# A scan and two MLPs in one kernel: the first units in another form, scores in quarters, a new opening order

## The chip, the cores and the metric

The kernel runs on one core of a Trainium2 chip. The metric is the device time of one execution in microseconds (us). The engines are named as in the profile: PE is TensorE, DVE is VectorE, ACT is ScalarE, POOL is GpSimd, SP is SyncE; SP issues the DMAs of this kernel.

## The reference

Four batches, eight heads, 768 time steps, 48 features a head. A gated linear scan is followed by two MLPs, each over 3072 tokens of 384 features with 2048 hidden features; everything is fp32.

```python
f = 1.0 / (1.0 + np.exp(-f_logit))
for t in range(S):
    state = f[:, :, t, :, None] * state + np.einsum('bhd,bhe->bhde', k[:, :, t], v[:, :, t])
    y[:, :, t] = np.einsum('bhd,bhde->bhe', q[:, :, t], state)
x = y.transpose(0, 2, 1, 3).reshape(B * S, H * D)
x = np.square(np.maximum(x @ w_in, 0)) @ w_out
h = x @ w_in2
out = (h * np.tanh(softplus(h))) @ w_out2
```

## The kernel before

**The scan** is cut into 12 chunks of 64 steps. A *unit* is one chunk of two of the four batches, so there are 24 units, two to a chunk; four units make a block of 512 tokens. Unit i and unit i + 2 follow each other in time, and the state goes from one to the next. The two batches of a unit are its two halves y; queries, keys and gates lie with features on the partitions, rows 64 to 111 for the one half and 0 to 47 for the other, and heads by time in the columns (8 x 64 = 512).

The steps of a unit, each a small function: load_j, load_f and load_v bring the gate logits, keys and queries, and values. v_min (L443), a_exp and a_ln (L446, L450), v_scan (L454) and a_dq, a_dk (L459, L464) make the decay factors. v_q (L469) scales the queries, one half at a time, into the tile mv; v_k (L473) scales the keys in place; v_end (L477) keeps the decay over the chunk. m_a (L488, L489) computes the scores, keys against queries, for 8 heads and 2 halves: 32 matmuls with 48 rows into a PSUM tile at. v_mask (L542) multiplies one half of them by the causal mask, into mv. m_t (L530) transposes the keys and a_kn (L552) copies them into kns, behind rows that hold a unit matrix (eye_kn, L651); thus one matmul takes the state and the new keys together. m_y (L567) makes the output y of the unit, features by tokens, in 64 matmuls; a_x (L603) rounds it to fp32r as the high part of x, v_x (L607) subtracts and keeps the rest as the low part. m_u (L577, L578) makes the new state, v_s (L593) scales it by the decay and puts it into the rows of the values tile vs of unit i + 2. From unit 9 on (QUAD) scores and states are made in another arrangement, quarters_a (L500, tile aq) and quarters_u (L511): two heads lie one above the other, so that four matmuls of 64 columns stand side by side, and the scores take two PSUM buffers; v_mask (L539) then takes four instructions of 64x4x64.

**The MLPs** work in fp32r with every operand split in a high and a low part, and three products (high by high, high by low, low by high). One step fc of 16 takes 128 hidden features of a block: l1 (L351) is 9 matmuls of 128x512 into an h buffer, act_a (L747, L748, L370) makes relu squared and its high part gh, act_b (L375) the low part gl, l2 (L362) is 9 matmuls into three accumulators. l2 of a step comes two steps of l1 later. There are 96 steps for each MLP; h_p has 5 PSUM buffers with the tag h, which l1, scores, y, states and transposed keys share. The weights of the first MLP come as 64-bit floats (load_w) and are turned by w_top or a_top, w_f (L271), w_hi (L292) and w_lo (L297). m_warm (L615) issues matmuls on constants into an accumulator.

**The order of the work.** Each engine works through its own list in the order in which the program issues instructions, and a semaphore holds it where it needs another engine. From the start to step 18 of l1 the order is the string START, a list of the functions above written by hand; hold makes the next load wait for the DVE instruction issued last. After that run(i) issues, for step i, what put(step, priority, function) has filed for it, sorted by priority, lower first. do_l1 has priority 100 and do_l2 120, v_x 13 and act_b 32 in the first 80 steps.

**The end.** Two sums tell whether the fast path is valid: set_flag_sum (L797 to L801, two small matmuls, a reduction and a comparison) writes flag. At the end every engine loads it (L90) and branches (L91) over a slow path that is not executed here. The results of the last block are stored by L880, L882 and L884.

Of the kernel before, what the change touches and what calls it, by code (L numbers as in the profile page):

```python
# [50 lines left out]
w_lo 1; do_l1 1; v_s 2 0; w_hi 2; act_a 0; w_f 3; w_lo 2; w_hi 3; act_b 0; hold; load_w 7; a_exp 4; w_lo 3; w_top 4;
w_top 5; hold; load_f 6; act_a 1; do_l1 2; w_f 4; a_ln 4; do_l2 0; v_s 2 1; act_a 2; w_f 5; hold; load_v 4; act_b 1;
v_s 3 0; hold; load_v 5; v_min 5; w_hi 4; v_s 3 1; do_l1 3; a_exp 5; w_lo 4; v_scan 4; a_top 6; act_b 2; w_f 6;
do_l2 1; w_hi 5; v_min 6; do_l1 4; w_lo 5; hold; load_f 7; do_l2 2; act_a 3; act_b 3; a_ln 5; act_a 4; w_top 8;
a_dq 4; do_l1 5; v_scan 5; do_l2 3; w_hi 6; a_top 7; v_q 4 0; a_dq 5; w_lo 6; act_b 4; hold; load_w 10; a_dk 4;
load_w 9; do_l1 6; w_f 7; a_dk 5; v_q 4 1; a_exp 6; w_hi 7; act_a 5; v_q 5 0; hold; load_v 6; do_l2 4; w_lo 7; v_k 4;
w_f 8; v_k 5; m_t 4; act_a 6; a_ln 6; w_hi 8; w_top 10; act_b 5; v_q 5 1; m_a 4; w_top 9; v_mask 4 1; w_lo 8; m_t 5;
do_l1 7; a_kn 4; m_a 5; act_a 7; v_min 7; v_end 5; v_end 4; v_scan 6; do_l1 8; a_dq 6; a_dk 6; v_mask 4 0; hold;
load_v 7; do_l2 5; m_u 4; a_exp 7; w_f 9; v_mask 5 1; a_kn 5; m_y 4; act_b 6; do_l2 6; w_f 10; act_a 8; v_mask 5 0;
a_ln 7; w_hi 10; v_s 4 0; w_hi 9; load_w 12; act_b 7; v_q 6 1; a_top 11; v_q 6 0; m_y 5; a_x 5; v_k 6; v_s 4 1; a_x 4;  # L60
# [917 lines left out]
```

## Time and profile before

| | |
|---|---|
| median of 3 runs | 885.54 us (885.53 to 886.3) |
| profiled execution, its own time | 883.13 us |
| its span | 881.3 us |
| PE busy | 867.0 us, 98% |
| DVE busy | 665.7 us, 76% |
| ACT busy | 634.0 us, 72% |
| POOL busy | 7.9 us, 1% |
| granted clock, mean | 0.997 |
| DMA | 90.79 MB, mean 103 GB/s |
| first group of L351 | starts at 34.18 us |
| last group, L872 | starts at 871.20 us |

Times in the views are us from the start of the span, of one profiled execution. Its own time is 1.8 us above its span, and 2.4 us below the median of the runs. Matmuls overlap: one of 512 columns is listed with 0.39 us, while nine that follow each other take 2.04.

### The profile page before, as it was taken

What the parts mean: (1) busy time and instruction counts of PE and PEld (TensorE: products, weight loads), DVE (VectorE), ACT (ScalarE), POOL (GpSimd) and SP (SyncE); (2) the same over time, 40 slices, a digit from 0 to 9 for tenths busy, and PEclk for the clock granted to TensorE, in tenths of its full rate; (3) what the DMA queues carried; (4) which work ended last, traced back from release to release, by engine and by line L of the source; (5) the groups of instructions that cost most, each with busy time, mean ns of one, the idle gap of its engine ahead of it and who ended that gap; (6) DMA issues with size and microseconds to landing.
All of it is one profiled execution on the core that took longest, in us unless ns stands there. A gap on an engine that the chain in (4) does not pass through costs nothing.

```text
span 881.3 us, 16421 instructions
## 1 busy us (share of the span) xinstructions
PE 867.0 (98%) x6543; PEld 707.9 (80%) x6543; DVE 665.7 (76%) x1133; ACT 634.0 (72%) x1161; POOL 7.9 (1%) x23
## 2 busy tenths in 40 slices
...
GB/s 279 342 182 217 85 46 76 229 129 230 167 147 214 150 220 148 147 95 73 250 193 59 72 0 1 73 1 0 72 1 6 67 0 18 56 0 33 5 1 39
DMA packets 30132, 90.79 MB, mean 103 GB/s; under 512 B 3680, under 2 KB 3680, under 8 KB 30048
## 3 DMA queue, kind: packets, MB, share of 16 engines
q1 hardware_dynamic: 30048, 89.67, 29.7%
q8 instruction: 53, 0.87, 0.4%
...
## 4 chain that ended last, share of the span: by engine, by line
PE 87%; DVE 5%; ACT 3%; DMA 3%; issue 1%; SPq 0%; DVEq 0%; ACTq 0%
PE h L351 40%; PE a L362 40%; PE y L567 2%; DMA in<-in_qkf_dram 2%; DMA sr<-in_w_dram 1%; PE at L488 1%; PE u L577 1%; DVE mv L469 1%; DVE es L454 1%; PE aq L500 1%; PE warm L615 1%; DVE gl L375 1%; PE uq L511 0%; DVE wbit L282 0%; ACT r L747 0%
## 5 line engine op out<-in xcount | busy, mean ns | idle before, releaser
L351 PE MATMUL h<-x,w 128*128 128x512 f32 x1728 | 423.4, 390 | 0.0
L362 PE MATMUL a<-gh,w 128*128 128x512 f32 x1146 | 386.0, 391 | 0.0
L351 PEld LDWEIGHTS h<-x,w 128*128 128x128 f32 x1728 | 323.8, 188 | 67.4
L362 PEld LDWEIGHTS a<-gh,w 128*128 128x128 f32 x1146 | 215.1, 188 | 45.7
L362 PE MATMUL a<-gl,w 128*128 128x512 f32 x573 | 223.9, 391 | 1.4 <-DVE gl L375 1.4
L814 ACT ACTIVATE e<-e 128x512 f32<-128x512 f32 x95 | 60.1, 632 | 116.1 <-DVE e L813 116.1
L362 PEld LDWEIGHTS a<-gl,w 128*128 128x128 f32 x573 | 107.6, 188 | 26.2 <-DVE gl L375 4.7
L375 DVE TENSOR_TENSOR gl<-r,gh 128x512 fp32r<-128x512 f32 x96 | 65.4, 683 | 81.6 <-ACT gh L370 81.2
L813 DVE TENSOR_SCALAR e<-h 128x512 f32<-128x512 f32 x95 | 65.7, 691 | 59.1 <-PE h L351 56.5
L747 ACT ACTIVATE r<-h 128x512 f32<-128x512 f32 x96 | 56.4, 587 | 47.5 <-PE h L351 47.4
L808 ACT ACTIVATE r<-u,cst 128x512 f32<-128x512 f32 x94 | 67.9, 722 | 8.6 <-DVE u L822 2.7
L822 DVE SCALAR_TENSOR_TENSOR u<-e 128x512 f32<-128x512 f32 x95 | 66.0, 695 | 10.0 <-ACT e L814 0.7
L375 DVE TENSOR_TENSOR gl<-g,gh 128x512 fp32r<-128x512 f32 x95 | 65.7, 692 | 0.2 <-ACT gh L370 0.2
L810 DVE TENSOR_TENSOR e<-h,u 128x512 f32<-128x512 f32 x94 | 64.3, 684 | 0.0
L817 DVE TENSOR_TENSOR g<-e,r 128x512 f32<-128x512 f32 x94 | 64.2, 683 | 0.0
L370 ACT ACTIVATE gh<-r 128x512 fp32r<-128x512 f32 x96 | 60.7, 632 | 3.1
L748 ACT ACTIVATE r<-r 128x512 f32<-128x512 f32 x96 | 60.7, 632 | 3.1
L370 ACT ACTIVATE gh<-g 128x512 fp32r<-128x512 f32 x95 | 60.1, 633 | 3.4 <-DVE g L841 0.8
L809 ACT ACTIVATE r<-r 128x512 f32<-128x512 f32 x94 | 59.5, 633 | 3.0
L522 ACT ACTIVATE kn<-kt 32x256 f32<-32x256 f32 (+1 forms) x104 | 37.6, 362 | 1.4
L607 DVE TENSOR_TENSOR x<-y,x 128x384 fp32r<-128x384 f32 x24 | 12.6, 552 | 28.1 <-ACT x L603 28.1
L454 DVE TENSOR_TENSOR_SCAN es<-es,cap 112x520 f32<-112x520 f32 x24 | 29.4, 1229 | 0.8 <-ACT es L450 0.8
(120 smaller groups left out, 662.3 us busy)
## 6 DMA issues: line engine op xcount, KB each, us to landing
...
```

The source lines that it names most:

```text
L351: T.matmul(out=ps, lhsT=w[:, k * 128:(k + 1) * 128], rhs=x[:, s, k], start=(i == 0), stop=(i == 8))
L362: T.matmul(out=acc[m], lhsT=w[:, m * 128:(m + 1) * 128], rhs=gx, start=(fc == 0 and i == 0), stop=(fc == FC - 1 and i == 2))
L370: A.activation(out=gh, in_=g, func=AF.Copy)
L375: V.tensor_tensor(out=gl, in0=g, in1=gh.bitcast(F32), op=ALU.subtract)
L748: A.activation(out=r, in_=r, func=AF.Square)
L808: A.activation(out=r, in_=u, func=AF.Ln, bias=two)
L809: A.activation(out=r, in_=r, func=AF.Exp, scale=-1.0)
L810: V.tensor_tensor(out=e, in0=hp, in1=u, op=ALU.mult)
L813: V.tensor_scalar(out=e2, in0=ps, scalar1=20.0, scalar2=None, op0=ALU.min)
L814: A.activation(out=e2, in_=e2, func=AF.Exp)
L817: V.tensor_tensor(out=g, in0=e, in1=r, op=ALU.mult)
L822: V.scalar_tensor_tensor(out=u2, in0=e2, scalar=2.0, in1=e2, op0=ALU.add, op1=ALU.mult)
```

## The change

Units 0 and 1 (FIRST) have no state before them. Their queries are scaled in one product of 112 rows, in place; scores are taken from there, with the halves at the rows of their own half, and one mask of 128x512 covers both. Their values are loaded into one half of vs with the rows of the halves exchanged; y comes out as tokens by features in 16 matmuls (early_y, tile ye), a copy a_y puts it into kts, and m_x transposes it in three pieces (tile xe). The new state takes 64 rows. Units 4 to 8 (SPLIT) take quarters_a and four masks. START is written anew: do_l1 0 stands ahead of m_u 2, other loads come in another order, the warm passes are fewer. v_x of units 10 and up goes to priority 28, act_b at steps 34, 50 and 66 to 9.5. The third store of the last block is issued by ACT, and set_flag_sum moves from step 42 of the second MLP to the end.

```diff
@@ -24,6 +24,8 @@
 NL = 5
 HC = 64
 QUAD = 9
+FIRST = 2
+SPLIT = 4
 PAIRS = 10
 EARLY = (
     (("kn0", -7), ("vs0", -4)),
@@ -38,37 +40,37 @@
 PH2 = {ENG.PE, ENG.DVE, ENG.Activation, ENG.Pool, ENG.SP}
 
 START = """
-m_warm 16; load_j 1; load_j 0; load_j 2; v_min 1; a_exp 1; a_ln 1; hold; load_f 1; load_f 0; v_min 0; load_j 3;
...
-m_u 2; v_x 3; a_x 2; v_x 2; hold; load_w 11; w_hi 1; load_w 6; a_top 3; m_u 3; load_w 8; do_l1 0; w_f 2; v_min 4;
...
+m_warm 14; load_j 0; load_j 1; load_f 0; v_min 0; a_exp 0; hold; load_j 2; load_f 1; a_ln 0; v_min 1; load_j 3;
...
+v_x 2; v_x 3; a_kn 2; w_f 1; w_hi 1; w_f 2; w_lo 1; hold; load_f 4; w_hi 2; load_w 8; do_l1 0; w_lo 2; m_u 2; w_top 3;
...
 """
 W_MIN = float(np.array(0x38000000, np.uint32).view(np.float32))
 W_MAX = float(np.array(0x47EFF000, np.uint32).view(np.float32))
@@ -436,7 +438,10 @@
             c, bp = divmod(i, 2)
             w = vs[i % 4]
             for y in range(2):
-                load(w[64 * y:64 * y + 64, y], vv[c, bp, y])
+                if i < FIRST:
+                    load(w[64 - 64 * y:128 - 64 * y, 0], vv[c, bp, y])
+                else:
+                    load(w[64 * y:64 * y + 64, y], vv[c, bp, y])
 
         def v_min(i):
             f = fkq(i)[0]
@@ -463,7 +468,11 @@
             e = es[i % 3][:, :, 1:]
             A.activation(out=e, in_=e, func=AF.Exp)
 
-        def v_q(i, y):
+        def v_q(i, y=None):
+            if i < FIRST:
+                q = fkq(i)[2]
+                V.tensor_tensor(out=q, in0=q, in1=fkq(i)[0], op=ALU.mult)
+                return
             r = (64, 0)[y]
             q4 = head(fkq(i)[2])
             V.tensor_tensor(out=mv[i % 2][r:r + 48, y], in0=q4[r:r + 48], in1=U[i]["eq"][r:r + 48], op=ALU.mult)
@@ -481,9 +490,18 @@
             V.tensor_tensor(out=fmin, in0=fmin, in1=U[i]["f"][:, :, 0], op=ALU.min)
 
         def m_a(i):
+            if i >= SPLIT:
+                return quarters_a(i)
             kt = head(fkq(i)[1])
             m = mv[i % 2]
             a = h_p.tile([128, H, C], F32, tag="h", name="at")
+            if i < FIRST:
+                q = head(fkq(i)[2])
+                for h in range(H):
+                    for r, o in ((64, 64), (0, 0)):
+                        T.matmul(out=a[o:o + 64, h], lhsT=kt[r:r + 48, h], rhs=q[r:r + 48, h])
+                U[i]["a"] = a
+                return
             for h in range(H):
                 T.matmul(out=a[0:64, h], lhsT=kt[64:112, h], rhs=m[64:112, 0, h])
                 T.matmul(out=a[64:128, h], lhsT=kt[0:48, h], rhs=m[0:48, 1, h])
@@ -530,10 +548,13 @@
                 T.transpose(tr[:, p], kt[:, 2 * p:2 * p + 2].rearrange("p h t -> p (h t)"), idn[0:112, 0:112])
             U[i]["tr"] = tr
 
-        def v_mask(i, y):
+        def v_mask(i, y=None):
             a = U[i]["a"]
+            if i < FIRST:
+                V.tensor_tensor(out=mv[i][:, 0], in0=a, in1=cmask.unsqueeze(1).to_broadcast([128, H, C]), op=ALU.mult)
+                return
             r = 64 * y
-            if i >= QUAD:
+            if i >= SPLIT:
                 o = mv[i % 2][r:r + 64, y].rearrange("p (a b) t -> p a b t", b=2)
                 for b in range(2):
                     V.tensor_tensor(out=o[:, :, b], in0=a[y][64 * b:64 * b + 64],
@@ -547,12 +568,32 @@
                 return
             tr = U[i].pop("tr")
             for y, r in ((0, 0), (1, 64)):
-                kv = kns[i % 2][r:r + 64, y].rearrange("p (a b) e -> p a b e", b=2)
+                k = vs[i][64 - r:128 - r, 1, :, 0:D] if i < FIRST else kns[i % 2][r:r + 64, y]
+                kv = k.rearrange("p (a b) e -> p a b e", b=2)
                 for s in range(2):
                     A.activation(out=kv[:, :, s], in_=tr[64 * s:64 * s + 64, :, 64 - 64 * y:112 - 64 * y],
                                  func=AF.Copy)
 
+        def early_y(i):
+            y = h_p.tile([128, H, D], F32, tag="h", name="ye")
+            for h in range(H):
+                for b in range(2):
+                    k = slice(64 - 64 * b, 128 - 64 * b)
+                    T.matmul(out=y[64 * b:64 * b + 64, h], lhsT=mv[i][k, 0, h], rhs=vs[i][k, 0, h, 0:D])
+            U[i]["y"] = y
+
+        def a_y(i):
+            A.activation(out=kts[i][:, 0:DM], in_=U[i].pop("y").rearrange("p h e -> p (h e)"), func=AF.Copy)
+
+        def m_x(i):
+            x = h_p.tile([128, 3, 128], F32, tag="h", name="xe")
+            for k in range(3):
+                T.transpose(x[:, k], kts[i][:, 128 * k:128 * k + 128], idn)
+            U[i]["x"] = x
+
         def m_y(i):
+            if i < FIRST:
+                return early_y(i)
             m, s = mv[i % 2], vs[i % 4].rearrange("p y h c -> p y (h c)")
             x = h_p.tile([128, 3, 2, C], F32, tag="h", name="y")
             groups = [[] for _ in range(4)]
@@ -573,7 +614,10 @@
                 return
             sv, kn = vsv(i), kns[i % 2]
             u = h_p.tile([128, H, D], F32, tag="h", name="u")
-            for h in range(H):
+            for h in range(H if i < FIRST else 0):
+                for r in (64, 0):
+                    T.matmul(out=u[r:r + 48, h], lhsT=vs[i][r:r + 64, 1, h, 0:D], rhs=vs[i][r:r + 64, 0, h, 0:D])
+            for h in range(H if i >= FIRST else 0):
                 T.matmul(out=u[64:112, h], lhsT=kn[0:112, 0, h], rhs=sv[0:112, 0, h])
                 T.matmul(out=u[0:48, h], lhsT=kn[0:128, 1, h], rhs=sv[0:128, 1, h])
             U[i]["u"] = u
@@ -636,8 +680,7 @@
         for i in range(4):
             if i < 2:
                 G.memset(kns[i][32:64, 1], 0.0)
-                G.memset(vs[i][64:128, 0], 0.0)
-                G.memset(vs[i][0:64, 1], 0.0)
+                G.memset(vs[i][0:64, 1, :, D:HC], 0.0)
             else:
                 G.memset(vs[i][64:112, 0, :, D:HC], 0.0)
                 G.memset(vs[i][0:32, 1, :, D:HC], 0.0)
@@ -707,7 +750,7 @@
                 put(s + 3, 11 - odd, v_mask, i, 1)
             put(end, 110, m_y, i)
             put(end + 1, 12, a_x, i)
-            put(end + 1, 13, v_x, i)
+            put(end + 1, 28 if i >= PAIRS else 13, v_x, i)
             if i < NU - 2:
                 put(s + 1, 50, load_f, i + 2)
                 put(s + 1, 50, load_v, i + 2)
@@ -757,7 +800,7 @@
         for i in range(n1):
             if i:
                 put(i, 5, act_a, i - 1)
-                put(i, 17 if i > last else 32, act_b, i - 1)
+                put(i, 17 if i > last else 9.5 if i in (34, 50, 66) else 32, act_b, i - 1)
             put(i, 100, do_l1, i)
             if i >= 2:
                 put(i, 120, do_l2, i - 2)
@@ -765,7 +808,7 @@
             act_a(n1 - 1)
             act_b(n1 - 1)
 
-        ops = (v_min, a_exp, a_ln, v_scan, a_dq, a_dk, v_q, v_k, v_end, v_fmin, m_a, m_t, v_mask, a_kn, m_y, m_u,
+        ops = (v_min, a_exp, a_ln, v_scan, a_dq, a_dk, v_q, v_k, v_end, v_fmin, m_a, m_t, v_mask, a_kn, m_y, a_y, m_x, m_u,
                a_x, v_x, v_s, load_j, load_f, load_v, load_w, w_top, a_top, w_f, w_hi, w_lo, do_l1,
                do_l2, act_a, act_b, m_warm, eye_kn, hold)
         ops = {f.__name__: f for f in ops}
@@ -881,15 +924,13 @@
             V.tensor_copy(out=ts[1], in_=acc[1])
             nc.sync.dma_start(out=dst(1), in_=ts[1])
             A.activation(out=ts[2], in_=acc[2], func=AF.Copy)
-            nc.sync.dma_start(out=dst(2), in_=ts[2])
+            A.dma_start(out=dst(2), in_=ts[2])
 
         st = None
         for i in range(6 * FC):
             b, fc = divmod(i, FC)
             if i == 40:
                 set_flag()
-            if i == 42:
-                set_flag_sum()
             if b < 5 and fc == 4:
                 load_x2(b + 1, at2)
             if b < 5 and fc in (8, 10, 12):
@@ -908,6 +949,7 @@
         for f in queue:
             f()
         last_l2(accs.pop(5), *tail)
+        set_flag_sum()
 
     with ExitStack() as c1:
         stages.append(c1.enter_context(tc.tile_pool(name="stg", bufs=2)))
```

The change has 42 more lines than the kernel before, so L469 is L478 there, L473 is L482, L542 is L563 (and L554 for units 0 and 1), L454 is L459, L443 is L448, L375 is L377, L607 is L651.

DVE in the opening, from the first scaling on; mv holds scaled queries or masked scores, in and early are the inputs of units 0, 1 and 2, 3. Before:

```order
L469 TENSOR_TENSOR mv_155<-in_145 48x512 x2
L473 TENSOR_TENSOR in_145<-in_145,es_162 112x512
L473 TENSOR_TENSOR in_144<-in_144,es_161 112x512
L443 TENSOR_SCALAR early_147<-early_147 112x512
L469 TENSOR_TENSOR mv_154<-in_144 48x512
L542 TENSOR_TENSOR mv_155<-at,cmask 64x512
L469 TENSOR_TENSOR mv_154<-in_144 48x512
L454 SCALAR_TENSOR_TENSOR es_163<-es_163,cap 112x520
L454 SCALAR_TENSOR_TENSOR es_161<-es_161,cap 112x520
L542 TENSOR_TENSOR mv_154<-at,cmask 64x512
L542 TENSOR_TENSOR mv_155<-at,cmask 64x512
```

Four products of 48 rows and, up to here, three masks of 64 rows; a fourth follows. The same stretch with the change:

```order
L482 TENSOR_TENSOR in_144<-in_144,es_161 112x512
L474 TENSOR_TENSOR in_144<-in_144 112x512
L474 TENSOR_TENSOR in_145<-in_145 112x512
L482 TENSOR_TENSOR in_145<-in_145,es_162 112x512
L448 TENSOR_SCALAR early_147<-early_147 112x512
L554 TENSOR_TENSOR mv_154<-at,cmask 128x512
L459 SCALAR_TENSOR_TENSOR es_163<-es_163,cap 112x520
L554 TENSOR_TENSOR mv_155<-at,cmask 128x512
L459 SCALAR_TENSOR_TENSOR es_161<-es_161,cap 112x520
```

Two query products of 112 rows and two masks of 128 rows stand for eight instructions; unit 0 comes first, and its key product ahead of its query product.

DVE around the low part of g that step 29 of l2 takes; x<-y is v_x of units 10 and 11, the rows on in, es and mv belong to units 12 and 13. Before:

```order
L375 TENSOR_TENSOR gl<-r,gh 128x512
L481 TENSOR_TENSOR fmin<-fmin,f 112x8
L607 TENSOR_TENSOR x<-y,x 128x3x128 x2
L454 SCALAR_TENSOR_TENSOR es_162<-es_162,cap 112x520
L469 TENSOR_TENSOR mv_154<-in_144 48x512 x2
L473 TENSOR_TENSOR in_144<-in_144,es_161 112x512
L375 TENSOR_TENSOR gl<-r,gh 128x512
```

The scan and three products stand behind v_x and ahead of the second gl. With the change:

```order
L377 TENSOR_TENSOR gl<-r,gh 128x512
L490 TENSOR_TENSOR fmin<-fmin,f 112x8
L459 SCALAR_TENSOR_TENSOR es_162<-es_162,cap 112x520
L478 TENSOR_TENSOR mv_154<-in_144 48x512 x2
L482 TENSOR_TENSOR in_144<-in_144,es_161 112x512
L651 TENSOR_TENSOR x<-y,x 128x3x128 x2
L377 TENSOR_TENSOR gl<-r,gh 128x512
```

The two low parts of x have moved behind the scan and the products.

SP at the end; before, the flag was loaded in the second MLP and only the branch is left here:

```order
L389 DMA x_8084<-x2d_96 128x1536
L385 DMA out_dram<-ot 128x512 x3
L880 DMA out_dram<-ot 128x512
L882 DMA out_dram<-ot 128x512
L884 DMA out_dram<-ot 128x512
L91 COMPARE_AND_BRANCH
```

With the change:

```order
L391 DMA x_8063<-x2d_96 128x1536
L387 DMA out_dram<-ot 128x512 x3
L923 DMA out_dram<-ot 128x512
L925 DMA out_dram<-ot 128x512
L92 TENSOR_LOAD flag
L92 ISA x2
L93 COMPARE_AND_BRANCH
```

One store has gone to ACT, and the load of the flag with its two following instructions has come between the stores and the branch.

## Rows read from the trace of the kernel before

**Rows 1.** Busy time by stretch: us, PE, PEld, DVE, ACT, POOL, clock, DMA share, GB/s

```profile
10.00:20.00 10.00, 8.71 (x206) 6.12 (x205) 9.80 (x15) 8.53 (x21) 0.00 (x0) 1.00 1.02 315
20.00:30.00 10.00, 8.27 (x209) 6.33 (x209) 9.22 (x16) 6.33 (x15) 0.00 (x0) 1.00 0.86 275
```

**Rows 2.** Chain that ended last, 0 to 36 us: start, duration, what

```profile
4.00 4.72 DMA in<-in_qkf_dram
...
19.20 1.39 issue
...
21.90 0.17 PE u L577
...
22.76 1.49 PE warm L615 x4
...
26.47 1.14 issue
...
28.92 1.03 PE y L567 x64
...
34.18 2.04 PE h L351 x8
```

**Rows 3.** Timeline of DVE, opening: start, us, line, operation, idle before and releaser

```profile
6.90 1.23 DVE L454 TENSOR_TENSOR_SCAN es<-es,cap 112x520 f32<-112x520 f32 x1
8.82 1.40 DVE L469 TENSOR_TENSOR mv<-in 48x512 f32<-48x512 f32 x2 [0.69 <-DMA in<-in_qkf_dram]
...
33.18 0.56 DVE L607 TENSOR_TENSOR x<-y,x 128x384 fp32r<-128x384 f32 x1 [1.24 <-ACT x L603]
33.66 0.95 DVE L271 SCALAR_TENSOR_TENSOR wbit<-r,top 128x768 uint32<-128x768 uint32 x1
```

**Rows 4.** Groups of DVE by line and form, 0 to 36 us: busy, mean ns

```profile
L542 DVE TENSOR_TENSOR mv<-at,cmask 64x512 f32<-64x512 f32 x8 | 5.4, 686 | 0.2
```

**Rows 5.** DMA of the first 36 us: what was moved, and the mean

```profile
DMA packets 2931, 10.50 MB, mean 292 GB/s; under 512 B 376, under 2 KB 376, under 8 KB 2926
```

**Rows 6.** Timeline of PE: scores of unit 5, and of unit 9

```profile
62.97 0.27 PE L488 MATMUL at<-mv,early 48*64 48x64 f32 x1
...
64.05 2.34 PE L351 MATMUL h<-x,w 128*128 128x512 f32 x9
...
129.43 0.69 PE L500 MATMUL aq<-mv,in 48*64 48x64 f32 x32
130.05 0.50 PE L362 MATMUL a<-gh,w 128*128 128x512 f32 x1
```

**Rows 7.** Timeline of PE at step 33 of l2

```profile
203.57 0.39 PE L362 MATMUL a<-gh,w 128*128 128x512 f32 x1
204.54 0.50 PE L362 MATMUL a<-gl,w 128*128 128x512 f32 x1 [0.58 <-DVE gl L375]
204.88 0.64 PE L362 MATMUL a<-gh,w 128*128 128x512 f32 x2
```

**Rows 8.** Waits: who on whom, us in total, times, longest; PE's alone below

```profile
DVE x L607 <- ACT x L603: 28.1, 11, 4.5
...
PE a L362 <- DVE gl L375: 1.4, 3, 0.6
```

**Rows 9.** Timeline of DVE ahead of the gl of step 29

```profile
180.28 1.02 DVE L607 TENSOR_TENSOR x<-y,x 128x384 fp32r<-128x384 f32 x2 [3.94 <-ACT x L603]
```

**Rows 10.** Timeline of all engines, from 870 us

```profile
873.18 0.69 DVE L881 COPY ot<-a 128x512 f32<-128x512 f32 x1 [1.24 <-PE a L872]
...
875.31 0.65 SPq L884 DMA_DIRECT2D out_dram<-ot  x1
```

**Rows 11.** Line L90 by engine (ns min, median, max); SP's own waits from 870 us

```profile
L90 DVEq TENSOR_LOAD <-flag x1: 542/542/542, 873.2 to 873.2; - x1
...
SPq L91 <- SPq L91: 2.9, 1, 2.9
```

**Rows 12.** The page's DMA queues: packets, MB, share of 16 engines

```profile
q8 instruction: 53, 0.87, 0.4%
```

More of the change, by code (lines that the diff above doesn't have):

```diff
@@ L51 @@
[L51 to L60, printed above, removed]
@@ L61 @@
-m_a 6; v_end 6; m_t 6; load_f 8; w_lo 9; v_scan 7; w_f 11; a_dq 7; v_x 4; w_hi 11; act_b 8; w_lo 10; v_mask 6 1;
-v_mask 6 0; do_l1 9; v_min 8; do_l2 7; do_l1 10; act_a 9; load_v 8; load_w 13; a_exp 8; v_x 5; a_ln 8; act_b 9;
-a_kn 6; a_top 12; load_w 15; load_w 14; v_q 7 0; w_lo 11; m_u 5; v_q 7 1; m_y 6; a_dk 7; v_scan 8; v_s 5 1; v_k 7;
-v_end 7; a_x 6; do_l2 8; a_dq 8; a_dk 8; do_l1 11; act_a 10; v_q 8 0; v_s 5 0; v_q 8 1; m_a 7; load_v 9; v_k 8; m_u 6;
-v_end 8; load_v 10; m_t 7; v_x 6; w_f 12; act_a 11; load_f 9; a_top 13; m_t 8; w_hi 12; w_top 14; m_a 8; a_kn 7;
@@ L66 @@
-load_f 10; do_l2 9; v_mask 7 0; a_kn 8; w_f 14; v_mask 7 1; w_lo 12; act_b 10; m_y 7; v_s 6 1; w_f 13; v_s 6 0;
-do_l2 10; w_hi 13; a_top 15; v_min 9; v_mask 8 1; do_l1 12; m_u 7; act_b 11; v_mask 8 0; a_x 7; a_exp 9; w_f 15;
-v_x 7; do_l2 11; w_lo 13; a_ln 9; w_hi 15; act_a 12; do_l1 13; w_hi 14; act_b 12; w_lo 14; v_scan 9; m_u 8; a_dq 9;
-a_dk 9; v_s 8 1; w_lo 15; act_a 13; v_end 9; do_l1 14; act_b 13; v_k 9; do_l2 12; do_l1 15; v_s 7 0; v_s 7 1;
-do_l2 13; m_y 8; act_a 14; act_b 14; v_s 8 0; do_l1 16; act_a 15; v_q 9 1; do_l2 14; act_a 16; act_b 15; a_x 8;
@@ L71 @@
-v_q 9 0; v_x 8; do_l1 17; act_a 17; act_b 16; act_b 17; do_l2 15; do_l1 18; do_l2 16
+m_warm 14; load_j 0; load_j 1; load_f 0; v_min 0; a_exp 0; hold; load_j 2; load_f 1; a_ln 0; v_min 1; load_j 3;
+load_v 0; v_scan 0; a_exp 1; a_ln 1; a_dq 0; hold; load_f 2; hold; load_v 1; v_scan 1; load_w 1; v_min 2; a_dk 0;
+a_dq 1; v_k 0; m_t 0; a_exp 2; hold; load_f 3; v_q 0; v_end 1; v_q 1; hold; load_w 0; m_a 0; hold; load_w 2; a_dk 1;
+v_k 1; m_a 1; a_ln 2; v_min 3; a_kn 0; a_exp 3; v_end 0; a_ln 3; v_mask 0; v_scan 2; v_mask 1; m_t 1; m_u 0; a_dq 2;
@@ new lines @@
+a_dk 2; m_y 0; v_scan 3; a_kn 1; a_dq 3; a_dk 3; v_q 2 1; a_y 0; v_q 2 0; m_warm 5; m_u 1; hold; load_v 2; hold;
+load_w 5; a_top 1; v_s 0 0; eye_kn 0; m_y 1; eye_kn 1; m_warm 4; m_x 0; a_top 0; v_k 2; v_k 3; v_q 3 0; v_s 0 1;
+v_q 3 1; m_a 2; v_s 1 0; hold; load_v 3; a_x 0; m_t 3; hold; load_w 3; v_s 1 1; m_a 3; v_mask 2 1; a_y 1; w_f 0;
+v_mask 2 0; v_x 0; v_end 3; v_mask 3 0; m_x 1; v_mask 3 1; a_kn 3; a_x 1; v_x 1; hold; load_w 4; w_hi 0; m_warm 3;
+m_y 2; a_top 2; load_w 9; load_f 6; w_lo 0; m_y 3; m_t 2; a_x 2; m_u 3; load_f 5; v_end 2; load_w 6; load_w 7; a_x 3;
@@ new lines @@
+a_ln 7; a_dk 6; do_l1 9; w_f 11; load_w 13; m_y 4; act_b 8; w_hi 11; v_k 6; m_y 5; v_scan 7; m_u 4; w_hi 10; m_t 6;
+v_s 4 1; do_l2 8; a_x 4; w_lo 10; act_a 9; w_lo 11; do_l1 10; a_top 12; act_b 9; a_kn 6; a_dq 7; a_top 13; v_x 4;
+v_q 6 0; a_x 5; w_f 12; do_l2 9; v_s 4 0; v_x 5; v_q 6 1; do_l1 11; w_hi 12; a_dk 7; m_a 6; v_end 6; m_u 5; w_lo 12;
+v_q 7 1; w_f 13; load_f 8; w_top 14; act_a 10; v_k 7; do_l1 12; v_end 7; a_top 15; act_b 10; w_hi 13; act_a 11;
+v_mask 6 1; v_q 7 0; w_lo 13; v_s 5 1; do_l2 10; do_l1 13; v_min 8; v_s 5 0; v_mask 6 0; act_a 12; act_b 12; m_y 6;
@@ new lines @@
+a_exp 8; w_f 14; m_a 7; load_v 8; a_ln 8; load_v 7; w_hi 14; act_b 11; v_scan 8; w_lo 14; v_mask 7 0; act_a 13;
+a_dq 8; m_t 7; a_dk 8; v_q 8 1; a_x 6; load_f 9; v_k 8; load_v 9; v_end 8; do_l2 11; a_kn 7; w_f 15; v_x 6; do_l1 14;
+do_l2 12; m_u 6; act_a 14; v_mask 7 1; v_q 8 0; w_hi 15; m_t 8; m_a 8; load_v 10; m_y 7; act_b 13; v_min 9; load_f 10;
+a_kn 8; w_lo 15; a_exp 9; v_s 6 0; do_l2 13; v_mask 8 1; v_s 6 1; v_mask 8 0; a_x 7; do_l1 15; v_x 7; a_ln 9;
+v_scan 9; act_b 14; a_dq 9; act_a 15; a_dk 9; m_u 8; m_y 8; a_x 8; m_u 7; do_l1 16; v_s 7 0; v_s 8 1; v_x 8; v_q 9 1;
```

19 lines of the change are left out of this document (11 added, 8 removed).

## The prediction

> **What bounds the kernel now.** I read the table of busy shares first (PE 98% of the span, DVE 76%, ACT 72%), then the chain that ended last. It is one row of TensorE work from 34.18 us, the first group of L351 [rows 2], to the last group of L872, which starts at 871.20. Nine matmuls of 512 columns take 2.04 us [rows 2]. From 34.18 on nothing counts but what TensorE does between these groups and the places where it waits. Before 34.18 it is otherwise: in the stretches 10 to 20 and 20 to 30 us DVE is busy 9.80 and 9.22 of 10 [rows 1], while PE's own 8.71 and 8.27 are partly warm passes and stalls. The opening is DVE's queue, read in order of time [rows 3]: it starts on its long run at 8.82, after a DMA wait of 0.69, and ends with the last low part of x at 33.74 (33.18 + 0.56), which releases L351. So there are three accounts: DVE's queue until the first L351, TensorE's list after it, and the tail.
>
> **The opening.** Units 0 and 1 scale their queries in two products of 112 rows instead of four of 48 rows, and mask in two of 128 rows instead of four of 64 rows. The elements in a row stay 512, and I take a product's time from its columns: a 48-row one takes 0.70 (1.40 for two, rows 3), a 64-row mask 0.686 [rows 4]. Two and two go: 2 x 0.70 + 2 x 0.686 = 2.77 us. w_f 1, 0.95 us (as the weight product at 33.66, rows 3), now stands behind the last v_x instead of ahead of it. DVE's queue between its start and the first L351 holds otherwise the same scans, key products, state updates, low parts and w_lo 0. Together -3.72.
>
> The start: v_q 1 waited for f1, which had been held back until the first v_min and landed at 8.72 (4.00 + 4.72, rows 2). load_f 0 is now issued without a hold, right behind j 0 and j 1. What is left ahead of the first product is unit 0's own chain. In the old order the first scan ended by 6.90, where the second starts [rows 3], and two exponentials on ACT follow it; an estimate of 8.4 for the first key product, between 7.8 and 8.8. I take -0.4, bounds -1.0 and 0.
>
> The one large idle time on DVE, 1.24 us ahead of v_x at 33.18 [rows 3], is a wait for m_y 2 and its copy, behind a PE that had itself stood still for 1.14 us at 26.47 with nothing to wait for [rows 2]. In the new order m_y 2 and m_y 3 again come last, but w_lo 0 and the low parts of units 0 and 1 fill DVE meanwhile; what is left is m_y 3 (1.03, rows 2), its copy and its low part. I take 0.8 us of idle in place of 1.24: -0.4, bounds -1.2 and +1.4.
>
> Sum of the opening: -3.7 - 0.4 - 0.4 = **-4.5**, first L351 near 29.7. The loads must keep up: 7.1 MB lie ahead of v 3 in the new list of loads (it was 7.1 MB to w 3 in the old one). The mean of the first 36 us is 292 GB/s [rows 5]; at it 7.1 MB take 24.3 us from 0.8 on, so v 3 comes at 25 to 27, and m_y 3, copy and low part (1.03 + 0.56 + 0.56, a copy of the same size put at the time of the low part) then end at 27.2 to 29.2. This path is as long as DVE's; so I go no lower than -5.8 and no higher than -1.5.
>
> y of units 0 and 1 by 64x48 results and three transposes is at most dearer on PE than 1.03 each, by an estimate of 0.3, plus one ACT copy of about 0.55 per unit. I cost both at nothing: they lie beside DVE's queue. If that cover were gone, they would cost 1.7 us.
>
> **TensorE's list after the first L351.** Four terms.
>
> *Scores in quarters.* For unit 5 the old form runs from 62.97 to 64.05, 1.08 us; for unit 9 the form in quarters, the same 32 matmuls with four side by side, runs from 129.43 to 130.05, 0.62 us [rows 6]. 0.46 us for each of units 4 to 8, all behind 34.18: **-2.3**. DVE gets four masks for two on such a unit; one of them costs at least half of 0.686 and at most all of it, so 0 to +1.4 us a unit; DVE has room behind 70 us, and I cost it at nothing. Scores take two of the five h buffers where they took one; that is a rival below.
>
> *m_u 2* now stands behind the first L351: **+0.86** (21.90 to 22.76, rows 2).
>
> *The low part of g.* TensorE waits three times for L375's gl, 1.4 us in all [rows 8]. In one, step 33, gl starts 0.97 behind gh where 0.23 is the pace, and the next group 0.34 behind that [rows 7]: 0.74 + 0.11 = 0.85; the other two, at 184.41 and 222.96, give 0.60 and 0.77 by the same reading. They are DVE's doing: v_x stands at priority 13, ahead of the scan and the products of the next units, and waits for ACT's copy, 28.1 us over 11 places [rows 8]. At 180.28 it has waited 3.94 [rows 9]; the scan, three products and then gl come after it and gl is late at 185. With v_x at 28 the scan and the products run in that idle time and gl follows v_x at once; for step 33 it is act_b itself that moves up, from 32 to 9.5. **-2.2**, bounds 0 and -2.9 (smaller waits further on).
>
> *set_flag_sum* leaves the middle: two tiny matmuls between groups of 512 columns. A group right behind small matmuls takes 2.34 instead of 2.04 [rows 6, 2]: **-0.3**.
>
> Sum: -2.3 + 0.86 - 2.2 - 0.3 = **-3.9**.
>
> **The tail.** The flag is now made behind the last matmul, and every engine must load it before it branches. DVE's load takes 0.54 [rows 11], which it used to do under the copy at 873.18 [rows 10]. Now two matmuls, a reduction and a comparison come first, an estimate of 0.6 us behind 873.6, then the load: DVE and PE branch some 1.2 later. SP loses the third store's 0.65 [rows 10] and gains a load of about the same length; behind its branch it stands 2.9 us [rows 11], waiting for nothing that a store sends. Between 0 (SP sets the end) and +1.3 (DVE or PE does), reached by -1 if a store did: **+0.7**. The third store from ACT saves issue time on SP and nothing else here. [...]
>
> **Sum.** -4.5 - 3.9 + 0.7 = -7.7. The profiled execution of 883.13 would become 875.4; it lies 2.4 below the median of the runs, so against 885.54 I say **877.8 us**.
>
> **The rivals.**
>
> *A: the opening gives back half.* PE stood still at 19.20 for 1.39 and at 26.47 for 1.14 [rows 2] without a releaser, while its instruction queue brought 53 packets, 0.87 MB in all [rows 12]. Before, the first of these lay in work with slack. The new list is shorter ahead of the first L351, and such a stop can fall into m_y 2 or m_y 3, on the path that ends last; with loads 1.5 to 2 us later than I have them it makes +3: **880.8**. For it: the load path is as long as DVE's. Against: the old DVE queue absorbed such stops with 1.24 of idle in all at the end. [...]
>
> *B: the middle is held up by buffers.* With two of five h buffers taken by scores until DVE has done four masks, TensorE could wait at each of units 4 to 8 as long as at step 33: 5 x 0.85 = +4.3, **882.1**. For it: DVE is busy 9.8 of 10 until 20 us and the new list asks for units 4 and 5 early. Against: the old kernel does the same from unit 9 on without a PE wait in the list of waits [rows 8].
>
> *C, the other side: the first L351 comes later than before.* Values for units 2 and 3 now come behind w 0, w 2 and w 5, 2.3 MB. If these loads crowd each other and the rate falls, m_y 3 slips with them. It decides from v 3 landing at 37 us, a mean below 195 GB/s: first L351 at 39.2, +9.5 against my sum, **887.3**, and more beyond. For it: two weights ahead of values. Against: 315 and 275 GB/s in the two stretches of the old opening [rows 1] under the same kind of queue.
>
> *D: the priorities do nothing*, because ACT's gh and not DVE's queue is late: -2.2 goes, **880.0**. Against it: at 184.4 gh is there, and TensorE waits for gl alone [rows 7].
>
> [...]
>
> **How the numbers follow.** Forecast 0.60; A 0.17; B 0.10; C 0.05; D 0.08. A measurement of this kernel tells 0.2%, 1.8 us, from no change. The forecast, A, D and most of B are faster: 0.92; 0.03 of B's and C's edges lies within 1.8 us; 0.05 slower. The range: low end with -5.8 in the opening, -2.9 for gl and a tail of 0, that is -5.8 - 4.6 = -10.4, 875.1, less 0.6 for the spread of runs: 874.5. The high end takes in A, D and B: 882.2.
>
> **What would show it.** Right: first L351 between 28.5 and 31.5; DVE's long run beginning before 8.82; masks of 128x512 in place of four of 64x512; scores of unit 4 in 0.62; no PE wait on gl at steps 29, 33, 37; v_x on ACT's copy well below 28.1 us; L872 starting near 862.8; an end 0.7 later behind the last matmul than now. Wrong: DVE idle in the opening on DMA or PE for more than 3 us (A or C), PE waits in front of aq or of L351 at units 4 to 8 (B), gl waits that stay (D), or a granted clock below 1.00 before 40 us.

## The result, and the profile after

The kernel with the change takes 875.42 us (median of 4 runs, 874.78 to 876.07) against 885.53 (4 runs, 884.53 to 886.3): a ratio of 0.9889, 95% interval 0.9874 to 0.9904. The forecast was 877.8, range 874.5 to 882.2. The profiled execution took 874.78 us (its span is 873.1), 8.35 less than the profiled one of before; the sum had said 7.7, and the two medians lie 10.1 apart. The rest of the distance to the forecast, some 1.7 us, is where the two profiled executions stand in their samples: that of before 2.4 below its median, that of after 0.6.

The three accounts of the prediction, read at the same places of both traces:

| | before | after | change | forecast |
|---|---|---|---|---|
| first group of L351 / L353 starts | 34.1 | 30.6 | -3.5 | -4.5 |
| from there to L872 / L915 | 837.1 | 831.4 | -5.7 | -3.9 |
| end of the last matmul of L872 / L915 to the end of the span | 7.7 | 8.6 | +0.9 | +0.7 |

They are read off PE's timelines, before and after; 34.11 is the timeline's time for the group that the chain puts at 34.18 [rows 2].

```profile
34.11 3.24 PE L351 MATMUL h<-x,w 128*128 128x512 f32 x13
...
871.20 0.98 PE L872 MATMUL a<-gh,w 128*128 128x256 f32 x6
```

```profile
30.62 2.36 PE L353 MATMUL h<-x,w 128*128 128x512 f32 x9
...
862.04 0.98 PE L915 MATMUL a<-gh,w 128*128 128x256 f32 x6
```

First the opening, on DVE's timeline of the kernel with the change:

```profile
8.26 0.68 DVE L482 TENSOR_TENSOR in<-in,es 112x512 f32<-112x512 f32 x1
...
10.90 0.69 DVE L474 TENSOR_TENSOR in<-in 112x512 f32<-112x512 f32 x1 [1.36 <-DMA in<-in_qkf_dram]
...
12.63 0.69 DVE L554 TENSOR_TENSOR mv<-at,cmask 128x512 f32<-128x512 f32 x1
...
19.22 0.69 DVE L482 TENSOR_TENSOR early<-early,es 112x512 f32<-112x512 f32 x1 [0.41 <-DMA early<-in_qkf_dram]
...
29.88 0.56 DVE L651 TENSOR_TENSOR x<-y,x 128x384 fp32r<-128x384 f32 x1 [0.78 <-ACT x L647]
```

The queue starts at 8.26 where it started at 8.82 [rows 3]; a mask of 128 rows takes the 0.69 of one of 64 rows [rows 4]; the wait ahead of the last low part is 0.78, as costed. New is the wait of 1.36 for f 1. On the chain of waits between 0 and 32 us a load stands at the end as well:

```profile
22.41 5.65 DMA vs<-in_vv_dram
28.06 0.14 issue
28.20 1.14 PE y L608 x64
```

v 3 landed at 28.06 and not at 25 to 27, and m_y 3 waited 1.4 us for it. DMA moved 351, 261 and then 410 GB/s, with the granted clock at 1.00 throughout (by stretch: us, PE, PEld, DVE, ACT, POOL, clock, DMA share, GB/s):

```profile
10.00:20.00 10.00, 9.54 (x210) 7.74 (x209) 8.47 (x13) 8.33 (x19) 0.00 (x0) 1.00 1.03 351
20.00:30.00 10.00, 7.49 (x219) 5.90 (x219) 8.99 (x15) 8.11 (x19) 0.00 (x0) 1.00 0.88 261
30.00:40.00 10.00, 9.45 (x98) 7.75 (x93) 9.91 (x14) 9.61 (x16) 0.00 (x0) 1.00 1.01 410
```

Then TensorE's list. Scores of unit 4 in quarters on PE's timeline:

```profile
65.20 0.69 PE L518 MATMUL aq<-mv,early 48*64 48x64 f32 x32
65.83 0.60 PE L548 MATMUL tr<-idn,early 112*128 112x112 f32 x4
```

0.63 us, as unit 9 had taken [rows 6]. The waits of the whole span, and below them PE's own from 29 us to the last group:

```profile
DVE x L651 <- ACT x L647: 10.4, 6, 3.8
...
PE u L621 <- ACT w L294: 0.6, 1, 0.6
```

In this list TensorE waits for gl nowhere any more, where it waited three times [rows 8]; v_x waits for ACT 10.4 us instead of 28.1. One wait is new: m_u 2 stands 0.6 us behind ACT. Give each matmul the time from its start to the start of the next one, from the first group to L915. Then the groups of 512 columns, with all waits behind them, shrank by 3.84 us (791.69 to 787.85), scores by 2.29, transposes and the flag's sums by 0.43, and states grew by 0.84.

### The profile page after: what moved, and what is told of

The parts are those of the page before. It is cut to its first block, busy times and chain, and to the rows that moved or that the text cites. A ratio compares the mean times of both kernels' runs of the same rounds, so it can differ in the third digit from the quotient of the medians.

```text
span 873.1 us, 16295 instructions
## 1 busy us (share of the span) xinstructions
PE 859.3 (98%) x6479; PEld 706.3 (81%) x6479; DVE 663.9 (76%) x1138; ACT 636.1 (73%) x1164; POOL 6.2 (1%) x21
## 3 DMA queue, kind: packets, MB, share of 16 engines
q1 hardware_dynamic: 29904, 89.41, 29.7%
## 4 chain that ended last, share of the span: by engine, by line
PE 96%; ACT 1%; DVE 1%; DMA 1%; issue 0%; ACTq 0%; DVEq 0%
PE h L353 44%; PE a L364 44%; PE y L608 2%; PE aq L518 1%; PE warm L659 1%; PE uq L529 1%; DMA vs<-in_vv_dram 1%; PE u L621 1%; PE tr L548 0%; ACT kn L694 0%; PE a L915 0%; ACT w L294 0%; ACT top L269 0%; ACT vs L574 0%; ACT early L464 0%
## 5 line engine op out<-in xcount | busy, mean ns | idle before, releaser
L353 PE MATMUL h<-x,w 128*128 128x512 f32 x1728 | 423.3, 389 | 0.0
L353 PEld LDWEIGHTS h<-x,w 128*128 128x128 f32 x1728 | 324.0, 188 | 67.5
L377 DVE TENSOR_TENSOR gl<-r,gh 128x512 fp32r<-128x512 f32 x96 | 65.4, 683 | 79.4 <-ACT gh L372 78.9
L377 DVE TENSOR_TENSOR gl<-g,gh 128x512 fp32r<-128x512 f32 x95 | 65.7, 692 | 0.0
L560 DVE TENSOR_TENSOR mv<-aq,cmask 64x256 f32<-64x256 f32 x80 | 33.7, 422 | 4.7 <-PE aq L518 3.3
L459 DVE TENSOR_TENSOR_SCAN es<-es,cap 112x520 f32<-112x520 f32 x24 | 29.6, 1232 | 1.0 <-ACT es L455 0.9
```

What stands on the lines that cost most here:

```text
L353: T.matmul(out=ps, lhsT=w[:, k * 128:(k + 1) * 128], rhs=x[:, s, k], start=(i == 0), stop=(i == 8))
L377: V.tensor_tensor(out=gl, in0=g, in1=gh.bitcast(F32), op=ALU.subtract)
```

## The experiments

Where no number of runs is given, an experiment is one execution. "T1" is the start of the first L353, "middle" the time from there to L915 (after: 30.62 and 831.42).

**Scores in halves again.** 

> Units 4 to 8 take their scores in halves again, everything else as with the change. Sum by terms: five units at 0.46 us on TensorE, so from the first L353 (30.6 us) to L915 the stretch grows from 831.4 to 833.7, span near 875.4. Rival (buffers): quarters also cost waits for h buffers or masks, which the halves give back; then the stretch grows by less than 1.5. First L353 and the end behind the last matmul stay within 0.2.

```diff
-SPLIT = 4
+SPLIT = 9
```

T1 29.29, middle 833.57: +2.15. Scores take 13.58 us in all instead of 11.32. PE's timeline of unit 4:

```profile
63.69 0.27 PE L506 MATMUL at<-mv,early 48*64 48x64 f32 x1
...
64.77 0.60 PE L548 MATMUL tr<-idn,early 112*128 112x112 f32 x4
```

1.08 against 0.63. T1 moved here too, and an early T1 by itself makes the middle longer, as the runs on the flag and on the loads show below (middles of 833.47 and 833.97, with the quarters in place). Counted from the first scores of unit 4 to L915, which leaves that out, the halves take 799.17 us and the quarters 796.83, 2.34 apart. The quarters are worth their matmul time and cost no waits; rival B falls.

**Both priorities back.** 

> v_x back to priority 13 and act_b to 32. Theory: all waits on gl were DVE's queue, the three large ones (2.2 us) and the small ones (1.3 us in the trace of before): L915 comes 3.5 later, and v_x waits for ACT's copy near 28 us again. Rival: the small waits went with the new order of the opening, +2.2. Rival D of the prediction: priorities do nothing, below +0.5.

```diff
-            put(end + 1, 28 if i >= PAIRS else 13, v_x, i)
+            put(end + 1, 13, v_x, i)
-            put(i, 17 if i > last else 9.5 if i in (34, 50, 66) else 32, act_b, i - 1)
+            put(i, 17 if i > last else 32, act_b, i - 1)
```

T1 30.43, middle 833.34: +1.9. The list of waits, and then one of two places on PE's timeline:

```profile
DVE x L651 <- ACT x L647: 22.5, 10, 4.5
```

```profile
327.74 0.39 PE L364 MATMUL a<-gh,w 128*128 128x512 f32 x1
328.59 0.50 PE L364 MATMUL a<-gl,w 128*128 128x512 f32 x1 [0.47 <-DVE gl L377]
```

The wait on ACT and the late gl are back, at other steps than before (197 and 328 us) and not all of them. From the first scores of unit 4 to L915 it is 799.30 against 796.83, +2.5.

**Only act_b back.** 

> Only act_b of steps 34, 50 and 66 back to 32; v_x stays at 28. Theory: step 33 of l2 waits 0.7 to 0.9 us for gl again and the two others 0.2 to 0.4, L915 0.9 to 1.5 later, the waits at steps 29 and 37 stay away. Rival: v_x alone frees them, below +0.3.

```diff
-            put(i, 17 if i > last else 9.5 if i in (34, 50, 66) else 32, act_b, i - 1)
+            put(i, 17 if i > last else 32, act_b, i - 1)
```

Middle 831.39, the same to 0.03, with T1 at 30.11, and no wait on gl. v_x alone frees them; the rival holds, and the sentence of the prediction on step 33 was wrong.

**The kernel before with both priorities.** 

> The kernel before with nothing but the two priorities (v_x 28 from unit 10 on, act_b 9.5 at three steps). Theory: first L351 stays at 34.1, L872 starts 3.5 earlier than 871.20, at 867.7, and no wait on gl is left above 0.2. Rival: only the three large waits go, 869.0; or they need the rest of the change, 871.

The edit is that of both priorities, the other way round, in the kernel before.

T1 34.90, L872 at 868.73: middle 833.83 against 837.09, -3.3. The groups of 512 columns with their waits take 788.28, 3.4 less than before, where the whole change has 787.85. The wait list has no gl in it, and v_x waits half as long:

```profile
DVE x L607 <- ACT x L603: 14.8, 6, 4.3
```

So the priorities carry 3.3 us by themselves, where I had priced three waits at 2.2; the smaller waits are the rest. The timelines bear this out. Add up how much later than the pace of 0.227 (2.04 by nine) every matmul on gl, and the one behind it, starts, wherever gl is more than 0.05 late: 6.03 us before and 2.76 in this run, 3.27 less; 2.46 with the change and 4.45 with both priorities back, 1.99 more. With the single undoing and the single doing at hand, the term is 1.9 to 3.3.

**The flag's sums back to step 42 of the second MLP.** 

> The flag's sums back to step 42 of the second MLP, the third store stays with ACT. Theory: from the last matmul of L915 to the end 8.6 us become 7.6 to 7.9, against 0.2 to 0.3 more in the middle: span 0.5 to 0.8 shorter. Rival: the engines' code at the end sets it, and where the flag is made does not matter: 0 to +0.3.

```diff
+            if i == 42:
+                set_flag_sum()
...
         last_l2(accs.pop(5), *tail)
-        set_flag_sum()
```

T1 28.75, L915 at 862.22, and 7.29 us from the last matmul to the end instead of 8.62. Another execution of the same kernel, the last experiment, had 7.16. With the flag at the end the tail is 8.62 to 9.31 in seven traces and 7.64 in one; with it at step 42 it is 7.16 to 7.60 in four. Making the flag last costs 1.3 us here (8.62 against 7.29). L915 comes 0.2 later than with the change although T1 is 1.9 earlier: an early T1 is not kept.

**The third store back on SP.** 

> Only the third store of the last block goes back to SP; the flag's sums stay at the end. Theory: SP's branch and what follows it set the end, so SP's extra issue of 0.4 to 0.65 us makes the end that much later. Rival: DVE's and PE's branch set it, no difference beyond 0.2.

```diff
-            A.dma_start(out=dst(2), in_=ts[2])
+            nc.sync.dma_start(out=dst(2), in_=ts[2])
```

Tail 8.67 against 8.62. SP's branch does come 0.6 later behind the last matmul (867.9 behind 865.53, where it was 866.2 behind 864.46), but SP then waits 2.8 us where it waited 3.5, and it does not set the end. Behind their branches the engines each issue an instruction DRAIN, and in every trace POOL goes on within 0.2 us of the last of them. The first of the two times in these lines is that of the DRAIN, on SP and on DVE: before, with the change, and with the store on SP.

```profile
L974 SPq DRAIN  x3: 7/7/13, 880.0 to 880.3; - x3
L974 DVEq DRAIN  x2: 10/72/134, 879.7 to 880.4; - x2
```

```profile
L1016 SPq DRAIN  x3: 7/7/13, 870.8 to 872.1; - x3
L1016 DVEq DRAIN  x2: 10/72/135, 871.7 to 872.1; - x2
```

```profile
L1016 SPq DRAIN  x3: 7/7/13, 871.8 to 873.2; - x3
L1016 DVEq DRAIN  x2: 10/73/136, 872.8 to 873.2; - x2
```

Before, SP came last. With the flag at the end DVE comes last, here and in the six other traces with a tail of 8.62 to 9.31, 5.7 to 6.3 us behind its branch; what it waits for there stays open. In the trace with 7.64 DVE took 3.9, and SP came last. So the rival holds, and with the flag at the end the store from ACT saves nothing. With the flag at step 42 SP comes last in two traces and DVE in two, at most 0.5 us apart, and there the store was not tried. What the store from ACT saves is the 0.6 us of SP's own time.

**f 1 ahead of j 2, v 3 ahead of w 5.** 

> f 1 ahead of j 2, and v 3 ahead of w 5. Theory: the opening lost the microsecond I had not counted to loads (f 1 at 10.8, v 3 at 28.1): DVE's wait of 1.36 on f 1 shrinks below 0.6, m_y 3 no longer waits 1.4 for v 3, and the first L353 starts at 29.3 to 29.9 instead of 30.62. Rival: DVE's own queue ends there anyway, first L353 at 30.4 to 30.7; or another load is late in turn.

```diff
-m_warm 14; load_j 0; load_j 1; load_f 0; v_min 0; a_exp 0; hold; load_j 2; load_f 1; a_ln 0; v_min 1; load_j 3;
+m_warm 14; load_j 0; load_j 1; load_f 0; v_min 0; a_exp 0; hold; load_f 1; load_j 2; a_ln 0; v_min 1; load_j 3;
...
-load_w 5; a_top 1; v_s 0 0; eye_kn 0; m_y 1; eye_kn 1; m_warm 4; m_x 0; a_top 0; v_k 2; v_k 3; v_q 3 0; v_s 0 1;
-v_q 3 1; m_a 2; v_s 1 0; hold; load_v 3; a_x 0; m_t 3; hold; load_w 3; v_s 1 1; m_a 3; v_mask 2 1; a_y 1; w_f 0;
+load_v 3; a_top 1; v_s 0 0; eye_kn 0; m_y 1; eye_kn 1; m_warm 4; m_x 0; a_top 0; v_k 2; v_k 3; v_q 3 0; v_s 0 1;
+v_q 3 1; m_a 2; v_s 1 0; hold; load_w 5; a_x 0; m_t 3; hold; load_w 3; v_s 1 1; m_a 3; v_mask 2 1; a_y 1; w_f 0;
```

T1 28.64. TensorE's wait on v 3 is gone, and DVE's on f 1 too, though it now waits 1.6 us for an input of units 2 and 3. T1 alone would not show that the loads held the opening, as it lies only 0.11 below the earliest of the traces with these loads untouched (28.75, with the flag at step 42); there f 1 and v 3 came in time by themselves, with waits of 0.4 and 0.2. And the middle grew to 833.97, and L915 came at 862.62, no earlier than with the change. On DVE's timeline, and in the list of PE's waits:

```profile
38.23 0.43 DVE L448 TENSOR_SCALAR in<-in 112x512 f32<-112x512 f32 x1 [2.77 <-DMA in<-in_qkf_dram]
```

```profile
PE h L353 <- DVE w L299: 1.3, 1, 1.3
```

v_min 6 waits for f 6, and behind it in DVE's queue stands w_lo 3, which a group of L353 needs. A first L353 two microseconds earlier meets weights that are not ready.

**That wait taken out of the queue** (with the flag at step 42): v 3 ahead of w 5, v_min 6 behind v_min 5. 

> Flag's sums at step 42; v 3 ahead of w 5, and v_min 6 behind v_min 5; f 1, j 2, f 4 and w 9 stay where the change has them. Theory: v_min 6, which waits for f 6 at the head of DVE's queue ahead of w_lo 3, is what held the groups after an early first L353; with it moved the first L353 is at 28.6 to 30 and the first aq at 63.0 to 64.5, L915 below 861.7, time 872.5 to 874. Rival: w 3 and w 4 come late in turn, as the same loads fill the queues; first aq at 64.9 to 66 as in the runs before, time not below 874.4.

```diff
-a_top 4; w_f 4; w_f 3; act_a 0; act_b 0; w_hi 4; w_hi 3; a_top 5; v_min 6; hold; load_w 14; v_s 3 1; w_lo 3; do_l1 1;
+a_top 4; w_f 4; w_f 3; act_a 0; act_b 0; w_hi 4; w_hi 3; a_top 5; hold; load_w 14; v_s 3 1; w_lo 3; do_l1 1;
...
-do_l1 4; a_top 6; v_s 2 1; w_f 6; w_hi 5; v_min 4; v_min 5; hold; load_v 6; act_a 3; w_hi 6; hold; load_w 15; do_l2 2;
+do_l1 4; a_top 6; v_s 2 1; w_f 6; w_hi 5; v_min 4; v_min 5; v_min 6; hold; load_v 6; act_a 3; w_hi 6; hold; load_w 15; do_l2 2;
```

T1 28.87, but the first aq at 64.89: the rival. The next load holds DVE now, f 4 in front of v_min 4, and the first gl behind 48.6 us starts 1.97 behind its gh, 1.7 late:

```profile
44.89 0.76 DVE L448 TENSOR_SCALAR early<-early 112x512 f32<-112x512 f32 x2 [1.63 <-DMA early<-in_qkf_dram]
```

874.27 us (6 runs), ratio 0.9881 (0.9860 to 0.9902). Over the seven traces that share the change's opening, T1 runs from 28.75 to 30.62, while the first scores of unit 4 start between 63.69 and 65.96 and hardly follow it: the trace with T1 28.75 has them at 64.87, that with 30.43 at 64.47. From 30 to 40 us the DMA share is 1.01 already with the change (the stretches above), and what comes early waits later.

**The order of more loads**, with the flag at step 42: f 1 ahead of j 2, v 3 ahead of w 5, v_min 6 later, f 4 in the place of w 9. 

> Flag's sums at step 42; f 1 ahead of j 2, v 3 ahead of w 5 as in the run on loads; v_min 6 moved behind v_min 5, and f 4 loaded in the place of w 9. Theory: after the first L353 the next bound is DVE's queue, where v_min 6 stands and waits for f 6 (2.8 us) ahead of w_lo 3; with that gone the first L353 stays near 28.7 and nothing waits up to the first aq, which comes at 62.7 to 63.5 instead of 64.5 to 66.0; L915 at 860.0 to 860.8, about 872.5 in time. Rival: w 3 or w 4 are late in turn, first aq at 64.5 or later, and it is no faster than the kernel with the flag alone.

The edits of the two runs above together, and:

```diff
-m_y 2; a_top 2; load_w 9; load_f 6; w_lo 0; m_y 3; m_t 2; a_x 2; m_u 3; load_f 5; v_end 2; load_w 6; load_w 7; a_x 3;
-v_x 2; v_x 3; a_kn 2; w_f 1; w_hi 1; w_f 2; w_lo 1; hold; load_f 4; w_hi 2; load_w 8; do_l1 0; w_lo 2; m_u 2; w_top 3;
+m_y 2; a_top 2; load_f 4; load_f 6; w_lo 0; m_y 3; m_t 2; a_x 2; m_u 3; load_f 5; v_end 2; load_w 6; load_w 7; a_x 3;
+v_x 2; v_x 3; a_kn 2; w_f 1; w_hi 1; w_f 2; w_lo 1; hold; load_w 9; w_hi 2; load_w 8; do_l1 0; w_lo 2; m_u 2; w_top 3;
```

874.44 us (5 runs), ratio 0.9885 (0.9868 to 0.9901). Its profiled execution, of 877.04, went another way than both theories. Chain of waits, then the stretch from 10 to 20 us:

```profile
9.68 1.69 issue
11.37 0.57 PE tr L548 x4
11.94 3.66 PE at L502 x64
```

```profile
10.00:20.00 10.00, 8.63 (x138) 7.61 (x139) 8.07 (x13) 8.40 (x20) 0.00 (x0) 0.66 1.01 344
```

v_min 2 stands ahead of the first key product and waited for j 2, which now came second. PE had nothing to do for 1.69 us after the warm passes, the granted clock was 0.69 from 10 to 15 us and 0.63 from 15 to 20, and T1 was 31.44. 64 matmuls of scores took 3.66 us; with the change 32 of them take 1.10.

**No warm passes between the first units.** 

> The three warm passes between the units of the opening are left out, the two ahead of it stay. Theory: they fill time in which PE waits anyway, granted clock 1.00 in every stretch, first L353 within 0.3 of 30.62. Rival: the granted clock falls after the pauses of PE, a group of nine takes up to 4.1 instead of 2.04, first L353 1 us or more later and the first groups longer.

`m_warm 5`, `m_warm 4` and `m_warm 3` are taken out of START. Busy time by stretch, columns as above:

```profile
20.00:25.00 5.00, 3.12 (x70) 2.50 (x64) 4.83 (x8) 4.91 (x13) 0.00 (x0) 1.00 1.02 296
25.00:30.00 5.00, 1.53 (x77) 1.40 (x81) 3.46 (x6) 2.14 (x3) 0.00 (x0) 0.79 1.02 279
30.00:35.00 5.00, 5.00 (x100) 4.32 (x93) 2.92 (x5) 3.33 (x9) 0.00 (x0) 0.52 1.02 415
```

The clock is still whole in the first stretch, 0.79 in the next and 0.52 in the one after. It fell inside a stop of TensorE of 2.93 us in m_y 2, from 26.53 on, with no releaser:

```profile
27.00:28.00 1.00, 0.00 (x0) 0.00 (x0) 0.97 (x3) 0.14 (x1) 0.00 (x0) 0.97 1.07 274
28.00:29.00 1.00, 0.00 (x0) 0.00 (x0) 0.53 (x1) 0.00 (x0) 0.00 (x0) 0.50 0.99 272
```

T1 was 34.02 and L915 came at 867.21, 5.2 later. The rival holds in this trace: the clock fell without the passes. But the stop is itself part of the 5.2, and one execution does not tell how much of the fall is due to the passes and how much to the stop.

**The new order with units 0 and 1 in the old form.** 

> The new order of the opening with units 0 and 1 in the old form (four query products, four masks, y in 64 matmuls, no copy and transposes of y). Theory: DVE's queue is 2.8 us longer ahead of the first L353; loads that were waited for hide about 1 of it, so first L353 at 30.5 to 32.5 where the runs of the new form had 28.8 to 30.6, and L915 1 to 2.5 later than the 861.5 to 863.1 of those runs. Rival (loads alone set it): first L353 within the spread of those runs and L915 within 863.1. Other rival: copies and unit matrices earlier on ACT make it worse, above 33.

`FIRST = 0`, four v_q and four v_mask, no a_y and m_x, unit matrices (eye_kn) ahead of a_kn 0, and vs zeroed as in the kernel before. T1 33.25, L915 at 864.02: the form, not only the order, is worth 2.6 us at T1 and 2.0 at L915 against the trace of after, 0.9 and 2.5 at L915 against two other traces with the same list behind the opening (863.11, 861.50). DVE waited 1.66 ahead of the last low part, and the chain shows why:

```profile
29.55 1.97 issue
```

PE stood still in the middle of m_y 3 with nothing to wait for. Part of the 2.6 is this stop and not the eight instructions; how much, one trace does not tell.

**The flag at step 42 in several runs.** 

> The kernel with the flag's sums back at step 42, timed. Theory: the tail of 8.6 to 9.3 us is 7.3, 1.3 less, the middle 0.2 more: about 1.0 below the kernel with the change, 874.4, and 0.987 to 0.989 of the kernel before. Rival: the gain lay within the spread of single runs, 875.4.

The edit is that of the experiment on the flag above.

874.36 us (6 runs, 872.91 to 878.27), ratio 0.9893 (0.9872 to 0.9913). The tail is 1.5 shorter in the trace, but the interval is that of the change itself. None of the three variants with several runs is shown to beat it.

## Why the prediction was right

In the main the traces show the mechanisms that were forecast, but the sum is better than its terms: the opening gave 1.0 less than forecast and the middle 1.8 more, and the two nearly cancel. That part is luck.

**The opening.** The forecast of 29.7 lies inside 28.75 to 30.62, the T1 of the seven traces with this opening; the profiled one is at the late end, by the wait on f 1 (1.36) and on v 3 (1.4). The wait on f 1 was not costed, that on v 3 only by the remark that the load path is as long as DVE's; with both, T1 stays inside the bounds of the sum. One half of rival A, late loads, is what this trace shows (v 3 comes 1.1 us behind the end of 25 to 27); the other half, a stop of PE in m_y 2 or m_y 3, is in the traces with the store on SP (1.5), the old form (1.97), the flag at step 42 in several runs (1.2) and without the warm passes (2.93). Counted in matmuls as the traces record them, these stops come at fixed places. Of the stops above 0.3 us with no releaser in the opening, before, after and in the experiments, all but one stand ahead of the 221st, the 346th or 347th or the 473rd matmul, whatever the work is there. (The one left is that of the run on more loads, where PE waited for DVE.) From one place to the next it is 126 matmuls, each with its weight load. In the trace of before the instruction queue [rows 12] brings one packet of 0.02 MB ahead of each of the two stops, one between 18 and 19 us and one between 25 and 26; that a late packet is what stops the engine no run shows. The step that did not hold is a silent one: that every microsecond at the first L353 goes to the end. The runs on loads show that it does not; with T1 of 28.6 and of 30.6 the first scores start within 0.2 us of each other (65.37 and 65.20).

**Quarters** -2.3: measured 2.29 in the trace, 2.15 to 2.34 by undoing them. **m_u 2** +0.86: 0.84, and a wait of 0.6 on ACT that I had not looked for. **The flag's sums out of the middle** -0.3: the reading was wrong and the size right by luck. It set 2.34 us of a timeline against 2.04 of a chain; the timeline before lists a group with nothing small ahead of it with 2.20, and the one behind the flag's sums with 2.35:

```profile
42.40 2.20 PE L351 MATMUL h<-x,w 128*128 128x512 f32 x9
...
648.42 2.35 PE L351 MATMUL h<-x,w 128*128 128x512 f32 x9
```

That is 0.15, and the sums themselves take 0.23 of the 0.43 by which they and the transposes shrank.

**gl** -2.2 was mis-sized: 3.3 by doing it alone, 1.9 by undoing it, and 3.6 by the count of late matmuls in the whole change (6.03 to 2.46). I had counted three waits that the list names, and had left the smaller ones, 0.12 to 0.18 late with 0.11 behind each, to the bound of -2.9, which they exceed. And the mechanism was v_x alone; act_b at step 34 does nothing measurable. Rival D falls.

**The tail** +0.7: +0.9 against before, 1.3 by undoing it. DVE makes the flag before any engine can load it. Its timeline, the line that loads the flag, and SP's own waits:

```profile
864.02 0.69 DVE L924 COPY ot<-a 128x512 f32<-128x512 f32 x1 [1.24 <-PE a L915]
...
864.96 0.14 DVE L844 TENSOR_SCALAR flag<-fmin 1x1 int32<-1x1 f32 x1
```

```profile
L92 DVEq TENSOR_LOAD <-flag x1: 801/801/801, 865.1 to 865.1; - x1
```

```profile
SPq L93 <- SPq L93: 3.5, 1, 3.5
```

The load starts at 865.1 where it started at 873.2 under the copy [rows 11], that is 0.7 behind the last matmul of L915 instead of 0.4 before its end, and takes 0.80 for 0.54. DVE's branch so comes 1.56 behind the last matmul instead of 0.19, and DVE overtakes SP at the end: the prediction's upper bound, +1.3 if DVE or PE sets the end, is the case that came. SP's wait behind its branch is 3.5 for 2.9, but SP no longer comes last. The low end of the range takes 0 for the tail and not the -1 of a store that sets the end; no run shows that 0: the tail was +0.9, and 8.67 with the third store back on SP where it is 8.62.

**The clock** did not fall with the change: it is 1.00 from 10 to 40 us. It fell without the three passes between the units, to 0.52 from 30 to 35 us, and L915 came 5.2 us later, the stop of 2.93 included; how much of that is the clock's stays open.

Rival C did not come: v 3 landed at 28.1, far from 37.
